# Gated linear attention and an MLP on one core: scores and running sums of two batches emitted as pairs, weights in 8 pieces instead of 12, k turned ahead of q, and a table that says which engine does each sum and copy

## The chip, the cores and the metric

The kernel runs on 1 core of a Trainium2 chip. The metric is the device time of one execution in microseconds (us). The time before is the median of 3 runs. A profile is one further execution, recorded instruction by instruction.

The engines are named as in the profile: PE is TensorE (matmuls), PEld its weight loads, DVE is VectorE, ACT is ScalarE, POOL is GpSimd, and SP is the engine whose queue issues nearly all DMAs here. SBUF is the on-chip memory of 128 partitions; PSUM holds matmul results and has 8 banks, all of which this kernel uses as one ring of eight buffers.

## What is computed

Two blocks in a row, all in float32 on the chip (the two weight matrices come as 64-bit floats and are turned into float32 by the kernel):

```python
# B, H, S, D = 4, 8, 768, 48
for t in range(S):                      # gated linear attention
    state = alpha[:, :, t, :, None] * state + k[:, :, t] (outer) v[:, :, t]
    y[:, :, t] = q[:, :, t] @ state     # 48 x 48 state per batch and head
x = y as (B, S, H * D)                  # 4 x 768 x 384
xn = (x - mean) / sqrt(var + 1e-6) * g_ln
out = x + max(xn @ w_ch1, 0) @ w_ch2    # w_ch1 384 x 1536, w_ch2 1536 x 384
```

## The kernel before

**Tiles and stages.** The 768 tokens are cut into 6 chunks of 128, so there are 24 pairs of chunk and batch. The function `attention(c, b)` does one of them: the logarithm of alpha (ACT), its running sum along the tokens as a matmul with a triangle of ones (tile `lps`, lines 330 and 335), two exponentials of it (ACT, lines 338 and 339), k and q multiplied by them (DVE, lines 341 and 343), both turned so that the head dimension lies on the partitions, the scores k·q (tile `aps`, lines 409 and 417), a masked copy of the scores (DVE, line 429), the update of the state (tile `ups`, line 445, then DVE line 458 and POOL line 460), the output (tile `yps`, line 481), the normalisation (ACT and DVE), and the turned result `xT` for the MLP. Chunk 0 works on whole 128-token blocks. The later chunks work on halves of 64 tokens, so that their matmuls are 64 wide or less and use one quarter of the TensorE array each: in a batch with an even number the two matmuls of a step use the two quarters off one diagonal, in an odd batch (`cross`) the quarters of the other one. For chunks 0 to 2, q and k are turned by TensorE (line 393, q first, then k, each followed by a copy, lines 398 and 400); from chunk 3 on by a DVE transpose and DMAs through DRAM.

**The MLP.** Chunk 0 uses plain matmuls: `hidden` (line 564, letters Y and Z of the order below, 12 column blocks `j` for each half of the batches) and `project` (line 576, letters P and Q). Chunks 1 to 5 use a scheme with fewer multiplications, in which sums of blocks are formed first: of the first weights (`combine_first`, line 802, letter S), of `xT` (`combine_x`, line 827, letter X), of the second weights (`combine_weights`, line 636, letter W) and of the hidden values (`combine_hidden`, line 663, letter N). All these sums are DVE instructions. The products are lines 853 and 676 (letters M and V); DVE, ACT and POOL add their results up.

**The weights.** They come in 12 pieces of 768 KB (6 of the first matrix, two column blocks `j` each; 6 of the second). A piece is loaded by one DMA (line 228) into one of `STAGED` = 3 staging buffers and turned into float32 in place by `round_weights`: three DVE instructions (lines 240, 242, 244), one of ACT (line 246), then DVE line 250 and either three of line 253 or one of line 256. When a piece is done, the load of piece i + 3 is issued. The letters A to L stand for the 12 pieces.

**What sets the order.** Every stage is a Python generator, and the string `ORDER` says which generator is advanced by one step next: small letters a to x are the 24 calls of `attention`, the capitals the rest. Instructions reach each engine's queue in exactly this order, and every engine, SP included, works through its queue in order. So an instruction that waits holds up all that stands behind it on its engine. In `ORDER` a batch with later chunks gives its scores in 8 steps of 2 matmuls (each float32 matmul is two TensorE instructions), and the string already mixes the steps of two batches in five of the ten pairs of batches.

```python
TURNED = 12
...
        lps = ps.tile([P, 512], FP32, name="lps", tag="bank", bufs=8)
...
    with tc.manual_schedule():
        for turn in ORDER:
            next(turns[turn], None)
```

## Time and profile before

| | us |
|---|---|
| median of 3 runs (lowest and highest) | 417.64 (416.98 to 420.2) |
| the profiled execution, whole | 418.43 |
| its span, first to last instruction | 416.6 |
| TensorE busy | 409.2 |
| VectorE busy | 344.8 |
| ScalarE busy | 182.4 |
| GpSimd busy | 151.1 |

A line of the timeline or of the chain of waits gives a start, a duration (both us) and what ran. In the timeline and in the groups, `xN` is the number of instructions, a pair like `128x512` is partitions by elements, and what stands in square brackets is how long the engine had been idle before and who ended that. "Busy" of TensorE is the time in which some matmul is under way; matmuls overlap, so a busy TensorE can still be waiting in part. The granted TensorE clock was 1.000 of full speed on average.

### The profile page before, as it was taken

Reading aid. Unit: us, or ns where it says so; the run is one execution under the profiler, and the core shown is the slowest. Engines: PE = TensorE matmul, PEld = TensorE weight load, DVE = VectorE, ACT = ScalarE, POOL = GpSimd, SP = SyncE. Lnnn points to the kernel's source line nnn. Section 1 sums busy time; section 2 is a strip of 40 time slices with the busy share of each in tenths; the row PEclk is TensorE's granted clock in tenths of the full one; section 3 lists DMA queues with packets and bytes.
Section 4 is the critical chain, followed back from the end, with each engine's and each line's share of the span. In section 5 each row is a group of like instructions: output and inputs, shape, how many; then the busy total and the mean of one; then the engine's idle time right before and its main releaser. Section 6 shows DMA issues by size and latency. Waiting matters only on the chain.

```text
span 416.6 us, 11605 instructions
## 1 busy us (share of the span) xinstructions
PE 409.2 (98%) x4628; PEld 363.2 (87%) x4628; DVE 344.8 (83%) x672; ACT 182.4 (44%) x460; POOL 151.1 (36%) x164
## 2 busy tenths in 40 slices
PE   7999899999999999999999999999999999999997
PEld 5888789866568889999889998889998899889996
DVE  3888979999999989998689779679687769857873
ACT  6599456955523585321754344174130640122300
POOL 1012020010012766026774141872136640667323
PEclk9999999999999999999999999999999999999999
DMA  8988985977866876537866785672026200100201
GB/s 266 278 258 231 254 248 151 282 228 171 231 138 152 248 163 118 123 78 189 177 135 151 184 215 146 107 170 61 24 72 171 54 24 2 57 20 1 77 19 57
DMA packets 127133, 59.69 MB, mean 143 GB/s; under 512 B 84540, under 2 KB 123196, under 8 KB 127080
## 3 DMA queue, kind: packets, MB, share of 16 engines
q1 hardware_dynamic: 126536, 58.79, 54.7%
q8 instruction: 36, 0.59, 0.6%
q10 hardware_dynamic: 544, 0.17, 0.2%
q14 instruction: 17, 0.14, 0.1%
HBM read 42.33 MB, written 16.61 MB: 141 GB/s over the span
## 4 chain that ended last, share of the span: by engine, by line
PE 88%; DMA 7%; DVE 2%; ACT 1%; SPq 0%; issue 0%; DVEq 0%
PE ops L676 31%; PE hps L853 31%; PE ops L576 8%; PE hps L564 7%; PE yps L481 4%; PE aps L417 3%; DMA gate<-row 2%; PE ups L445 2%; DMA vn<-in_v_dram 2%; DMA ws<-in_moe_w_ch_dram 1%; DMA kept<-x 1%; DMA ra<-in_alpha_dram 1%; PE lps L335 1%; PE xps L539 1%; PE tps L393 1%; ACT lps L339 0%
## 5 line engine op out<-in xcount | busy, mean ns | idle before, releaser
L692 POOL TENSOR_TENSOR ob<-ob,u 128x192 f32<-128x192 f32 x40 | 26.2, 666 | 69.9 <-DVE ob L689 55.5
L853 PE MATMUL hps<-sum,w 128*128 128x256 f32 x192 | 47.1, 380 | 0.0
L460 POOL TENSOR_TENSOR mid<-mid,gate 112x192 f32<-112x192 f32 x20 | 12.8, 643 | 86.5 <-DVE mid L458 47.4
L853 PEld LDWEIGHTS hps<-sum,w 128*128 128x128 f32 x192 | 36.3, 190 | 4.9
L676 PE MATMUL ops<-w,hT 128*128 128x192 f32 x224 | 40.4, 328 | 0.0
L676 PEld LDWEIGHTS ops<-w,hT 128*128 128x128 f32 x224 | 36.8, 190 | 0.5
L564 PE MATMUL hps<-xT,w 128*128 128x256 f32 x144 | 33.5, 383 | 1.8 <-DVE mid L458 1.8
L853 PE MATMUL hps<-xT,w 128*128 128x256 f32 x136 | 34.4, 380 | 0.0
L904 ACT ACTIVATE hT<-hT 128x512 f32<-128x512 f32 x48 | 27.9, 621 | 10.6 <-POOL hT L891 7.4
L576 PE MATMUL ops<-w,hT 128*128 128x384 f32 x96 | 32.4, 490 | 0.0
L564 PEld LDWEIGHTS hps<-xT,w 128*128 128x128 f32 x144 | 26.5, 190 | 5.5 <-issue 2.0
L853 PEld LDWEIGHTS hps<-xT,w 128*128 128x128 f32 x136 | 25.7, 190 | 3.5
L676 PE MATMUL ops<-ws,sum 128*128 128x192 f32 x160 | 28.6, 327 | 0.0
L576 PEld LDWEIGHTS ops<-w,hT 128*128 128x128 f32 x96 | 17.7, 190 | 11.4
L513 ACT ACTIVATE xn<-x,few 128x384 f32<-128x384 f32 x24 | 14.8, 615 | 28.6 <-DVE few L509 28.1
L676 PEld LDWEIGHTS ops<-ws,sum 128*128 128x128 f32 x160 | 26.4, 190 | 0.1
L676 PE MATMUL ops<-ws,hT 128*128 128x192 f32 x128 | 23.4, 326 | 0.0
L686 DVE TENSOR_TENSOR ob<-ops,ob 128x192 f32<-128x192 f32 x50 | 16.7, 349 | 7.3 <-PE ops L676 2.9
L676 PE MATMUL ops<-more,sum 128*128 128x192 f32 x120 | 21.9, 326 | 0.0
L676 PEld LDWEIGHTS ops<-ws,hT 128*128 128x128 f32 x128 | 21.3, 190 | 0.1
L460 POOL TENSOR_TENSOR st<-st,gate 112x192 f32<-112x192 f32 x16 | 10.6, 665 | 28.9 <-DVE st L458 28.9
L883 ACT COPY hT<-hps 128x512 f32<-128x512 f32 x8 | 4.7, 583 | 36.4 <-PE hps L853 36.4
(240 smaller groups left out, 1113.7 us busy)
## 6 DMA issues: line engine op xcount, KB each, us to landing
ws<-in_moe_w_ch_dram SPq DMA_DIRECT2D x12, 768.0 KB
vn<-in_v_dram SPq DMA_DIRECT2D x12, 384.0 KB
kept<-x SPq DMA_DIRECT2D x24, 192.0 KB
ob<-kept SPq DMA_DIRECT2D x24, 192.0 KB
rows<-rj SPq DMA_DIRECT2D x48, 96.0 KB
out_dram<-ob SPq DMA_DIRECT2D x19, 192.0 KB
ra<-in_alpha_dram SPq DMA_DIRECT2D x14, 192.0 KB
rk<-in_k_dram SPq DMA_DIRECT2D x6, 384.0 KB
```

The source lines that it names most:

```text
L417: nc.tensor.matmul(aps[0][halves[i if cross else 1 - i], p, s], kT[rs, p, s], qT[rs, p, s], start=True, stop=True)
L445: nc.tensor.matmul(up[h, p], qk_of(c, b)[ts, 1, p, i, :h.stop - h.start], vn[ts, i, p], start=True, stop=True)
L460: nc.gpsimd.tensor_mul(new, new, by)
L481: nc.tensor.matmul(yps[j][halves[s], i, p], of, by, skip_group_check=True, start=not (cross and k), stop=k == 1 or not cross)
L513: act(out=xn, in_=x, func=AFT.Square, bias=mean, accum_out=dev)
L564: nc.tensor.matmul(hps, w1[:, j // 2, f, j % 2 * P:][:, :P], xT_of[0][:, f, bs], start=(f == 0), stop=(f == NF - 1))
L576: nc.tensor.matmul(ops_of[b], hT_of[c][:, j, b], w2[:, j], start=(j == 0), stop=(j == NJ - 1))
L676: nc.tensor.matmul(acc, lhs[:, j], rhs[:, j], start=(j == 0), stop=(j == NT - 1))
L686: nc.vector.tensor_add(x, acc, x)
L692: getattr(nc.gpsimd, f"tensor_{op}")(x, x, y)
L853: nc.tensor.matmul(acc[:, i], w, b, start=True, stop=True)
L904: nc.scalar.activation(out=x, in_=x, func=AFT.Relu)
```

## The change

It has five parts.

1. **Pairs.** For chunks 1 to 5 the running sums of an even batch and the odd batch after it are emitted in one step (four quarter-array matmuls, eight TensorE instructions), and so are their scores (8 steps of four matmuls instead of 16 steps of two). Both batches' PSUM banks are taken at that step.
2. **Weights.** 8 pieces (`PIECES` = 4 for each matrix, three column blocks `j` each, 1,152 KB) instead of 12, with `STAGED` = 2 staging buffers instead of 3, each half as large again. `w1` is now one plain tile.
3. **Turning.** Where TensorE turns q and k, k comes first.
4. **Table.** `WHERE` gives, for each sum of W, N, X and S and for each batch's q multiplication and copies, which of two engines does it. For sums and the q multiplication 0 is DVE and 1 is POOL; for copies 0 is ACT and 1 is DVE. The ones: N 35 of 80, X 33 of 55, S 7 of 19, W 6 of 13; q multiplication 10 of 24.
5. **Order.** A new string of 1,539 letters instead of 1,646 (fewer steps and fewer pieces). Its first 39 letters are the old ones.

```diff
-STAGED = 3
+STAGED = 2
+PIECES = 4
 TURNED = 12
...
+WHERE = {
+    "N": "00000100011001011010000110110010100101100011101001010001011110100001000110101110",
+    "S": "1101100010001010000",
+    "W": "0100011110001",
+    "X": "1111011111101000001101100100010000111110101111101011110",
+    "a": "0100",
+    "b": "0100",
+    "c": "0100",
+    "d": "0001",
+    "e": "1100",
+    "f": "1000",
...
+def pick(marks, usual=0):
+    return int(marks.pop(0)) if marks else int(usual)
...
-    w1 = cpool.tile([P, NJ // 2, NF, 2 * P], FP32, name="w1")
+    w1 = cpool.tile([P, NF, DF], FP32, name="w1")
...
+    for i in range(PIECES):
+        cs = slice(i * DF // PIECES, (i + 1) * DF // PIECES)
+        pieces.append((w1[:, :, cs], w1_src[:, :, cs]))
+    for i in range(PIECES):
+        js = slice(i * NJ // PIECES, (i + 1) * NJ // PIECES)
         pieces.append((w2[:, js], w2_src[:, js]))
-    pieces = pieces[::2] + pieces[1::2]
...
         if whole:
-            nc.tensor.matmul(lps[:, :DM], tri, a, start=True, stop=True)
+            lps = ps.tile([P, 512], FP32, name="lps", tag="bank", bufs=8)
+            nc.tensor.matmul(lps[:, :DM], tri, las.pop((c, b)), start=True, stop=True)
+            yield
         else:
-            for h in range(2):
-                of = halves[1 - h if cross else h]
-                nc.tensor.matmul(lps[halves[h], :DM], tri[of, of], a[of], start=True, stop=True)
-        yield
+            if b % 2:
+                for o in (b - 1, b):
+                    sums[c, o] = ps.tile([P, 512], FP32, name="lps", tag="bank", bufs=8)
+                for o in (b - 1, b):
+                    for h in range(2):
+                        of = halves[1 - h if o % 2 else h]
+                        nc.tensor.matmul(sums[c, o][halves[h], :DM], tri[of, of], las[c, o][of],
+                                         start=True, stop=True)
+                yield
+            lps = sums.pop((c, b))
...
-        nc.vector.tensor_mul(qk[:, 0], raws.pop(("q", c, b)), eq)
+        (nc.vector, nc.gpsimd)[pick(marks)].tensor_mul(
+            qk[:, 0], raws.pop(("q", c, b)), eq)
...
-        for i in range(0 if turned(c, b) else 2):
+        for i in () if turned(c, b) else (1, 0):
...
+            if b % 2:
+                pair = [ps.tile([P, NP, 2, HS], FP32, name="aps0", tag="bank", bufs=8)
+                        for _ in range(2)]
+                scores[c, b - 1], scores[c, b] = pair
+                for p in range(NP):
+                    for s in range(2):
+                        for o in range(2):
+                            for i in range(2):
+                                rs = slice(64 * i, 64 * i + D)
+                                q_of, k_of = turned_of[c, b - 1 + o]
+                                nc.tensor.matmul(pair[o][halves[i if o else 1 - i], p, s],
+                                                 k_of[rs, p, s], q_of[rs, p, s],
+                                                 start=True, stop=True)
+                        if s == 0 or p + 1 < NP:
+                            yield
...
+    sides = {n: list(WHERE.get(n, "")) for n in "WNXS"}
+
+    def summer(name, op):
+        return getattr((nc.vector, nc.gpsimd)[pick(sides[name])], op)
...
-            op(o, x, y)
+            summer("N", op)(o, x, y)
```

More of the change, by code (lines that the diff above doesn't have):

```diff
@@ L17 @@
 EPS = 1e-6
-STAGED = 3
+STAGED = 2
+PIECES = 4
 TURNED = 12
 ORDER = (
-    "acacababcdaacabdbaabdcacabbacbbababceccbaAcfcdbadaacecacfeafdaddeedadbbbfccbeacc"
-    "fafddghdffbfcfeebbeAfefdhffaeebgeeeeeeAfbaAffbejbgdidedYcjchggifffeBdcCgAYYehdiY"
-    "ceeegghiighideefdfefhhdcghhiiiidghfhgghhcBghgghdhghBhghhgBgjggZZCZZZZYYjYCfZhifY"
-    "hkiDCBZfDDkiiCiijeiZYZklYYgggZkjYfjjjjkYkkYhjhijEZhEjiihkgljjjjjFEEFiijjFFZggZlZ"
-    "ZZZkeieiDliZlZlZlllZHZkliSklkehhhlIeilkSIklZkHljGgkllkggglfmjilkYGYYYYYYeYYejjhj"
-    "kkkjIlmGnkgGnOkYlHmmmkOHlQjnInmQSfikJJPlffPnnShJKlQKLgQnfmnhLpSfmlnKgiOLPWWWPWmh"
-    "SXoppSSooXkjSooQQQXnkkmmonXmnmnXmnniimnmnjjjSXmmnXSllnmiSOPmSmnnmpoOoPPMmppXoXmp"
-    "pmXnnnnSMSWWplnMMMMMlSMMSMMMMiMMMMXMMjlPmQlMMMMrmMMMiMOrqpppnWqoooprooppopomMppp"
-    "opqpqqMMMqqMjWlRWMjqnpMMMMRMMMMMMMMMMMMMMklRkRkkkmokWMMpMMMMRWMROrMqrrlRmRRRRorM"
-    "MMMMWMMMqooppsqmsmkNRqMqpqqqrqooooonnrOsNNNNqNKotNNNqqMosNMMMMMWoNqqNMMqMMNMMMMM"
-    "MMNpqrroMrrtttttrrrrrrrrrqoNtXtXsMMMXNXXMMXMMMXXrqqXsXMpmMMMMMsMoMoMXMMMMMMMMMMM"
-    "MMMMMppMmMMMRsMnvMMMMMnRRRuMMMtMOMMMMMMRMRMMMMMMnMMMMMMpvtspvttttotOstssttusssss"
-    "sssvRtsuttsotMMMuqqqMOrvMRpvvRMNpOMMvqMNMMMMssRssuuurRtrvsrrruRNNNNttMxNrNNMNMMM"
-    "MMMMMMrqMNNtMsNMMMMMMMMuNnMMMrMMMMwmvuuvrONNOvvuvuvvMuuuvvvuvsuwssssxuvvxwXXtuMX"
-    "XXXXMuXwMXuMMMMMsMXxtMMuttvtMwOXxxxqMMuxwuwwMMMMMwxrMMMMMMMMMMMMMMuuMMMMMMMMMMMM"
-    "MMMMtvvvvMvvRRMMMMMMMMMMMRRRMMMMxxwwxRRRRRxwvxwwxxwxwwwwwwxRxxuMMxMMRMMOsNNNNNNN"
-    "NNNNwttwwMxxxxwMMMMqMMMMMxMMMMMMMMMMNNqNNvNuMMMMuMMxxxXXXXXXXXXxMMMMMMXOMuMMxMXM"
-    "wMMMMMMMMMMMMMMMMMMMMMMMMMMMMMMMMMMMMMOOMOMMMMMMwwwwxwMMMMMMMMMMMMMMRRRRRRRuuRRR"
-    "RRNNNvNNNNwNNMMMMMMwXNMMMMNXXXXXXXXXMMMMMMMMMMMMMMMVMNMXONNVVVVVVVVVVVMVVVVVVVVV"
-    "VVVVVVVVVVLVVVVVVVVVVVVVVVVVVVVNNMVVVVVVVVVMRRMMMMMRRRRRRRRNRRNNMJOMMMMMMNNNNNNN"
-    "NMOMMMMMMOMMMMMMMMMMMMMMNNMMMNNMNMMMMMMMMMMMMM"
-)
@@ new lines @@
+    "acacababcdaacabdbaabdcacabbacbbababceccafdbccbbdafeeAdfabfddacccaeabaafaeeeebaef"
+    "ffdfdafcAdffffdffffdbbbbbgAhccAdcbhacbhggeddedBfcfccgYdhhgYdcAdYYhddYieeggejhehc"
+    "gegdedeYffjhecfjBjfjZZiiBZZZZhfBBjjjjjffhhhhhhhhhChhhggCgCYYlCeiZYZkiYZZZiiZDhZZ"
+    "iiYfYhljDjjjjjjjgjiejhhYgggYheiggEhEikDfYYlSShhgZhYYYieDkliYYYYlkefkYgkkZkggklll"
+    "lEgZiiiigllFFjSlllmjlEljllllOeefZZkijZZFZnGfZkjjZFjjnkhklmnQOmngngGhhlQkmSinmkHP"
+    "HXGHlSmSmffXXXninlpXnSSOPPPoPPPkPkWkkOmOlXpWWollllQllSWoOXXQQSXoooSSSnQSSXnnnnnn"
@@ new lines @@
+    "nnnkkkmpmmionpjQXnpnjpSWWMMMMjWnmnkMMMMMMMMmkpGMMMMqMMMMpmMmSQjoMrnrmmMrmrmrnMMk"
+    "MlMMMMrMMnWpjMMWRMMMMWqMMMMMMMMMWpRpRpppOppjpppipppmMMMkMppRMoRoRqMMMpMoqoqMiRRR"
+    "RoMMoMMRlqnnNMpNWNNqqNNOliMMMmMMMMMNNRWmNMMMMMMMMMNNNNMorrrMMMMMiMNMMMotrOsrNrrr"
+    "rrrmmMoNppqpoqqtpXqtMsXXXXnsXXoXMMoooopMssssMMMMMMtMXtttsppXMMMMMMMMMMXoMMMMMMMM"
+    "MMMMMMMrMMMqMMRRMMMMMMMMMMmMMMMMMMRRptnnRmtoqMMMMMMnMMuMOMrrqrvqqttttttOttttttRR"
+    "RRqRvNqqNNvqMqMMvvMMnNRMMsMMNNNNRtvruMoMsrtOurMMMMMMMMuNsrssutsMNtNvsrvuNtNvsxMM"
@@ new lines @@
+    "MMMNMuMNMMMMMNMMMwuXqrMsMXMMMXrMMXXXXXXxOvrvvxvvvvvvvvuquuuxrXrvqXrxxxxMMMMMMMMM"
+    "MwwwqMMMMMMwMMMMRMMMMMMMMMMMMMMMMMMMMMMMwwwMtttttvMMHMMMMMMMMMMRRRRRMRRRRMMvsxxx"
+    "xxxxNxxxxxsssusOONsxMMsMRMNMNNNNMwvtwOsMrvvvvrMNNNtRNvMMNMMMMMvMtMMMMxMMMMwxuxsw"
+    "uwuMwwwxNMuuNNNOxxwxXwwwuXXXXXXXMMXMXMMMMMMuuuMMMMMMMMMMMXxMMMMMvMMxMMMMMMMMMMMM"
+    "MRRRMMMMMMOuwvwOuMMMMMMMMRMMMMMMMMMMMMMMMMMMMxRRRxORMRRMMRwMRwNMNNNNNNMMMMMXMNMM"
+    "XXMMMXXXXXXNNNNMMMMMMMMNXXVVVVVVVVVVVVVVVVVVVVVVVVVVVVVVVVVVVVVVVVVVVVVVVVVVVMMM"
@@ new lines @@
+    "NNVVVVVVVVVRRNMRRMMMMMRRRRRRRRMMMMMMMNOMOMMNOMMOMNMNMMMMNNNNNNMNNMMMMMMMMMMMMMMM"
+    "NNNNMMMMMMMMMMMMMMM"
+)
+WHERE = {
[9 more added lines that the diff above has]
+    "f": "1000",
+    "g": "0000",
+    "h": "1001",
+    "i": "0001",
+    "j": "0000",
+    "k": "0000",
+    "l": "0010",
+    "m": "1",
+    "n": "1",
+    "o": "0",
+    "p": "0",
+    "q": "0",
+    "r": "1",
+    "s": "0",
+    "t": "0",
+    "u": "1",
+    "v": "1",
+    "w": "1",
+    "x": "1",
+}
@@ L214 @@
     pieces = []
-    for i in range(NJ // 2):
-        cs, js = slice(2 * i * P, 2 * (i + 1) * P), slice(2 * i, 2 * (i + 1))
-        pieces.append((w1[:, i], w1_src[:, :, cs]))
+    for i in range(PIECES):
[3 more added lines that the diff above has]
+        js = slice(i * NJ // PIECES, (i + 1) * NJ // PIECES)
         pieces.append((w2[:, js], w2_src[:, js]))
-    pieces = pieces[::2] + pieces[1::2]
     staged = {}
@@ L251, in round_weights @@
             op1=AOP.bitwise_or)
-        for f in range(NF) if i < NJ // 2 else ():
+        for f in range(NF) if i < PIECES else ():
             stt(out=dst[:, f], in0=dst[:, f], scalar=g_col[:, f:f + 1], in1=hi[:, f].bitcast(FP32),
                 op0=AOP.mult, op1=AOP.mult)
-        if i >= NJ // 2:
+        if i >= PIECES:
             stt(out=dst, in0=dst, scalar=2.0 ** -20, in1=hi.bitcast(FP32), op0=AOP.mult, op1=AOP.mult)
@@ L264, in take_weights @@
         else:
-            for f in range(NF) if i < NJ // 2 else ():
+            for f in range(NF) if i < PIECES else ():
                 nc.scalar.mul(pieces[i][0][:, f], pieces[i][0][:, f], g_col[:, f:f + 1])
@@ L304 @@
         nc.gpsimd.memset(at, 0.0)
-    x_of, xT_of, hT_of, las = ({} for _ in range(4))
+    x_of, xT_of, hT_of, las, turned_of, scores, sums = ({} for _ in range(7))
     def attention(c, b):
         whole, last = c == 0, c + 1 == NCB
+        marks = list(WHERE.get(chr(ord("a") + c * B + b), ""))
+        copies = (nc.scalar.copy, nc.vector.tensor_copy)
         cross = b % 2 and not whole
@@ L326, in attention @@
         yield
-        lps = ps.tile([P, 512], FP32, name="lps", tag="bank", bufs=8)
-        a = las.pop((c, b))
         if whole:
-            nc.tensor.matmul(lps[:, :DM], tri, a, start=True, stop=True)
-        else:
-            for h in range(2):
-                of = halves[1 - h if cross else h]
-                nc.tensor.matmul(lps[halves[h], :DM], tri[of, of], a[of], start=True, stop=True)
-        yield
+            lps = ps.tile([P, 512], FP32, name="lps", tag="bank", bufs=8)
+            nc.tensor.matmul(lps[:, :DM], tri, las.pop((c, b)), start=True, stop=True)
+            yield
+        else:
+            if b % 2:
[8 more added lines that the diff above has]
+            lps = sums.pop((c, b))
         lv = lps[:, :DM].rearrange("t (i p d) -> t i p d", i=2, d=D)
@@ L367, in turned_tiles @@
         def turned_tiles():
-            return [work.tile([R, NP, 2, HS], FP32, name=n, tag="sum", bufs=12)
-                    for n in ("qT", "kT")]
+            turned_of[c, b] = [work.tile([R, NP, 2, HS], FP32, name=n, tag="sum", bufs=12)
+                               for n in ("qT", "kT")]
+            return turned_of[c, b]
         if not turned(c, b):
@@ L396, in attention @@
             tv = tps.rearrange("r p (s t) -> r p s t", s=2)
-            if i:
-                (nc.vector.tensor_copy if whole else nc.scalar.copy)(out=kT, in_=tv)
-            else:
-                nc.scalar.copy(out=qT, in_=tv)
+            copies[pick(marks, whole and i)](out=kT if i else qT, in_=tv)
             yield
-        aps = [ps.tile([P, NP, 2, HS], FP32, name=f"aps{i}", tag="bank", bufs=8)
-               for i in range(2 if whole else 1)]
-        for p in range(NP):
-            if whole:
+        if whole:
+            aps = [ps.tile([P, NP, 2, HS], FP32, name=f"aps{i}", tag="bank", bufs=8)
+                   for i in range(2)]
+            for p in range(NP):
                 for i in range(2):
@@ L412, in attention @@
                                      start=True, stop=True)
-                continue
-            for s in range(2):
-                for i in range(2):
-                    rs = slice(64 * i, 64 * i + D)
-                    nc.tensor.matmul(aps[0][halves[i if cross else 1 - i], p, s],
-                                     kT[rs, p, s], qT[rs, p, s], start=True, stop=True)
-                if s == 0 or p + 1 < NP:
-                    yield
-        yield
+        else:
+            if b % 2:
+                pair = [ps.tile([P, NP, 2, HS], FP32, name="aps0", tag="bank", bufs=8)
+                        for _ in range(2)]
+                scores[c, b - 1], scores[c, b] = pair
+                for p in range(NP):
+                    for s in range(2):
[8 more added lines that the diff above has]
+                            yield
+        if whole or b % 2:
+            yield
         if whole:
@@ L430, in attention @@
                 out=at.rearrange("k p s t -> k (p s) t"),
-                data=aps[0].rearrange("k p s t -> k (p s) t"),
+                data=scores.pop((c, b)).rearrange("k p s t -> k (p s) t"),
                 mask=mask_of_halves.unsqueeze(1).broadcast_to([P, 2 * NP, HS]))
@@ L540, in attention @@
         yield
-        nc.scalar.copy(out=xT_of[c][:, :, b], in_=xps)
+        copies[pick(marks)](out=xT_of[c][:, :, b], in_=xps)
         yield
@@ L563, in hidden @@
         for f in range(NF):
-            nc.tensor.matmul(hps, w1[:, j // 2, f, j % 2 * P:][:, :P], xT_of[0][:, f, bs],
+            nc.tensor.matmul(hps, w1[:, f, j * P:(j + 1) * P], xT_of[0][:, f, bs],
                              start=(f == 0), stop=(f == NF - 1))
@@ L616, in weights_ready @@
         return win["b"]
+    sides = {n: list(WHERE.get(n, "")) for n in "WNXS"}
+    def summer(name, op):
+        return getattr((nc.vector, nc.gpsimd)[pick(sides[name])], op)
     def combine_weights():
-        spare = [stage.tile([P, NF, 2 * P], INT64, name="ws", tag="ws") for _ in range(3)]
+        spare = [stage.tile([P, NF, NF * P], INT64, name="ws", tag="ws") for _ in range(STAGED)]
         spare = [t.rearrange("p a c -> p (a c)").bitcast(FP32) for t in spare]
         new = [t[:, i * NT * HM:][:, :NT * HM].rearrange("p (j m) -> p j m", m=HM)
-               for t in spare for i in range(2)] + [
+               for t in spare for i in range(3)] + [
             more[:, i].rearrange("p (j m) -> p j m", m=HM) for i in range(4)]
@@ L625, in combine_weights @@
         t8, t9, t12, t1, n0, n6, n2, n13, n5, n10 = new
-        add, sub = nc.vector.tensor_add, nc.vector.tensor_sub
+        add, sub = "tensor_add", "tensor_sub"
         ready = weights_ready()
@@ L635, in combine_weights @@
                 ((13,), sub, n13, t8, b[4])):
-            op(o, x, y)
+            summer("W", op)(o, x, y)
             ready |= {n: o for n in ns}
@@ L650, in combine_hidden @@
             work.tile([P, NT, P], FP32, name=f"sum{i}", tag="sum", bufs=12) for i in range(6))
-        add, sub = nc.vector.tensor_add, nc.vector.tensor_sub
+        add, sub = "tensor_add", "tensor_sub"
         for n, op, o, x, y in (
@@ L662, in combine_hidden @@
                 del ready[old]
-            op(o, x, y)
+            summer("N", op)(o, x, y)
             ready[n] = o
@@ L757, in product, with w1_block @@
         yield
+    def w1_block(t, f):
+        return w1[:, f, t * NT * P:(t + 1) * NT * P].rearrange("p (a c) -> p a c", a=2)
     def first_weights_ready():
         if "a" not in first_of:
-            first_of["a"] = {n: [w1[:, 2 * t:2 * t + 2, f]]
+            first_of["a"] = {n: [w1_block(t, f)]
                              for n, t, f in ((7, 2, 1), (10, 1, 0), (13, 0, 1), (8, 0, 0))}
@@ L780, in combine_first @@
         extra = cpool.tile([P, 6 * P], FP32, name="extra")
-        a = [[w1[:, 2 * t:2 * t + 2, f]] for t in range(3) for f in range(NF)]
+        a = [[w1_block(t, f)] for t in range(3) for f in range(NF)]
         spare = [raw.tile([P, 2, 2, NP, D], FP32, name=f"r{n}", tag="in", bufs=6).rearrange(
@@ L785, in combine_first @@
         n9, n1 = ([x[:, 4 * P:].unsqueeze(1) for x in spare[2 * i:2 * i + 2]] for i in range(2))
-        add, sub = nc.vector.tensor_add, nc.vector.tensor_sub
+        add, sub = "tensor_add", "tensor_sub"
         ready = first_weights_ready()
@@ L801, in combine_first @@
             for o, u, w in zip(out, parts(x, len(out)), parts(y, len(out))):
-                op(o, u, w)
+                summer("S", op)(o, u, w)
             if n is not None:
@@ L817, in combine_x @@
         t101, t103, t100, m7, t102, m10, m9, m13, m8 = new[:9]
-        add, sub = nc.vector.tensor_add, nc.vector.tensor_sub
+        add, sub = "tensor_add", "tensor_sub"
         ready = x_ready(c)
@@ L826, in combine_x @@
                 (8, sub, m8, t102, b[1])):
-            op(out, x, y)
+            summer("X", op)(out, x, y)
             if n is not None:
```

## Prediction, made before the changed kernel was run

> **What bounds the kernel now.** I read the page's busy times first, then TensorE's waits, then the chain of waits in order of time, and then the timeline at the places that the change touches.

> ```profile
> PE 409.2 (98%) x4628; PEld 363.2 (87%) x4628; DVE 344.8 (83%) x672; ACT 182.4 (44%) x460; POOL 151.1 (36%) x164
> PE hps L564 <- DVE mid L458: 1.8, 1, 1.8
> PE tps L393 <- DVE qk L343: 1.3, 1, 1.3
> PE lps L276 <- DVE more L273: 1.1, 1, 1.1
> PE aps L409 <- ACT qT L400: 0.2, 1, 0.2
> ```

> TensorE is busy for 98% of the span, and all its waits come to 4.4 us, each at one place. Nothing else can be the bound: VectorE has 72 us to spare, GpSimd 265. So time can only come from TensorE's own work, from those 4.4 us, and from work that goes badly together on the array. The last can be read from the chain (start, duration, what):

> ```profile
> 86.02 0.64 PE lps L335 x4
> ...
> 108.95 0.81 PE lps L335 x8
> ...
> 116.04 1.09 PE aps L417 x64
> ...
> 141.02 0.87 PE aps L417 x35
> ...
> 213.18 0.74 PE aps L417 x26
> ...
> 279.45 1.08 PE aps L417 x60
> ```

> The blocks of 60 and 64 are two batches whose steps the order already mixes: 17 to 18 ns for one instruction. The blocks of 26 and 35 are a batch by itself: 28 and 25 ns. Running sums by themselves take 0.64 us for one batch, 0.81 us for two. Each change between full-array and quarter-array matmuls also costs:

> ```profile
> 115.55 0.49 PE L576 MATMUL ops<-w,hT 128*128 128x384 f32 x1
> 115.97 1.16 PE L417 MATMUL aps<-qT,kT 48*64 48x64 f32 x64
> ```

> The block starts 0.42 us after the matmul before it, where 384 columns follow each other every 0.32 us (40 in 13.10 us, chain at 87.13): 0.1 us. Back again, starts in the trace show 0.1 us at the last small matmul and 0.1 at the first big one. One change is 0.15 us on average.

> **The change part by part**, against the profiled execution (418.43 us: span 416.6 and 1.8 around it, 0.8 above the median of the three runs, 417.64).

> *Scores as pairs.* The same 640 instructions. Five of ten pairs are mixed already. For the other five, 320 instructions at 26.5 less 17.5 ns give 2.9 us. But the old order puts single running sums between single scores, on the other diagonal of the array: at 178.27 to 179.25, 32 scores and 4 sums take 0.98 us, and at pair prices they would take 32 x 17.5 ns + 0.81/2 = 0.97. Nothing is to be had there. Group by group (starts in the trace against pair prices) the excess is 0.7 us at 25 to 29, 0.4 at 32, 0.6 at 139, 0.1 to 0.2 in five others: 2.4 in all, part of it waits. I take -2.0, ends 0 and -2.9. In this the running sums are neutral: five single pairs of them would save 5 x (1.28 - 0.81) = 2.4 if they stood alone, and cost 5 x 0.81 = 4.0 if the old ones were wholly hidden; 178.27 says in the middle.

> *The order.* Expanding both strings step by step, TensorE changes between full and quarter array 52 times before and 46 times after: 6 x 0.15 = -0.9 (ends -0.5 and -1.2).

> *k ahead of q.* At 9.78 TensorE waits 1.3 us for line 343, the multiplication of q, which stands behind that of k (0.56 us, from 8.33; q from 9.17). Turning k needs the first alone. In the first chunk k's copy is on DVE and q's on ACT as before. -0.5 (ends 0 and -0.6). Late next: the scores still need both copies.

> *Weights, first piece.* Its rounding on DVE and ACT before:

> ```profile
> 25.07 0.54 DVE L240 TENSOR_SCALAR w<-ws 128x768 int32<-128x768 int32 x1
> 25.64 0.96 DVE L242 SCALAR_TENSOR_TENSOR w<-ws,w 128x768 f32<-128x768 uint32 x1
> 26.63 0.56 DVE L244 TENSOR_SCALAR ws<-ws 128x768 int32<-128x768 int32 x1
> 27.65 0.48 DVE L519 TENSOR_SCALAR xn<-x,few 128x384 f32<-128x384 f32 x1 [0.46 <-ACT few L516]
> 28.57 0.96 DVE L250 SCALAR_TENSOR_TENSOR ws<-ws 128x768 int32<-128x768 int32 x1 [0.44 <-ACT ws L246]
> 29.66 1.28 DVE L253 SCALAR_TENSOR_TENSOR w<-w,small,ws 128x256 f32<-128x256 f32 x3
> ```

> It is done at 30.94, and the first hidden product starts at 30.60 on the part that is ready. The piece had landed at 21.3 by the semaphore records, so 3.7 us lay between. A piece half as large again takes 3.1 us instead of 2.1 on the DMA engines (the second one came 2.1 us after the DMA ahead of it), and on SP's queue its issue moves behind the second gate column and the row of batch d (0.4 and 0.5 us): it lands at about 23.4, when VectorE comes to it. Its chain grows from 5.9 to about 8.4 us, so it is done at 31.8. The first product stands at the same place of TensorE's work (priced by the rows above, 22.4 us after the first running sum, as before), so it would start at 30.5. Also the normalised x of batch b (line 519) now stands behind the piece's first three instructions, and TensorE turns it just before. I take +1.2, ends 0 and +4.

> *The wait of 1.8 us at 43.9.* TensorE waits for a PSUM bank there: the multiply-out of a state sum (line 458) that frees it stands on DVE behind the second piece's rounding, and that had waited for its load (landed 39.8). In the new order the second piece's load is issued ahead of d's k, q and v work, it has 15 us until the next column blocks need it, and no bank is taken at that place within 1.2 us of its release. -1.8 (ends -1.8 and 0).

> *Weights, later pieces.* 24 DVE instructions and 4 of ACT fewer, but VectorE has time to spare: 0. The second matrix is wanted earlier: `project` needs all of its last third some 7 us sooner in TensorE's work than before, and by the same reckoning (4.4 us load and 1.05 more, a chain of 8.4) the seventh piece is done about when it is wanted, at 98 us. +0.7, ends 0 and +3.

> *The table.* On VectorE a sum of 128x512 takes 0.68 us, of 128x256 0.42, on GpSimd 128x512 takes 1.27 and 128x192 0.59; between these lie about 0.73 for 256, 1.0 for 384, and beyond them 1.8 for 768 elements (estimates on the straight line through these two rows). VectorE loses 35 x 0.68 + 33 x 0.42 + 7 x 0.68 + 6 x 0.95 + 10 x 0.57 = 54 us, GpSimd gains 35 x 1.27 + 33 x 0.73 + 7 x 1.27 + 6 x 1.8 + 10 x 1.0 = 98 and stands at 249 of 416. Neither is a bound. But they hinder each other:

> ```profile
> 375.90 1.28 POOL L878 TENSOR_TENSOR at<-ra,rq 128x512 f32<-128x512 f32 x1
> 377.25 1.60 POOL L879 TENSOR_TENSOR at<-at,at 128x512 f32<-128x512 f32 x1
> 376.18 1.55 DVE L663 TENSOR_TENSOR sum<-sum,hT 128x512 f32<-128x512 f32 x1
> 377.76 1.64 DVE L663 TENSOR_TENSOR sum<-sum,sum 128x512 f32<-128x512 f32 x1
> ```

> The 0.68 us sums took 1.55 and 1.64 beside GpSimd. What is queued behind a GpSimd sum is the state's multiplication (line 460), which the output matmuls need. The distances in the order between a sum and its product are as before (1.3 us at the least in both). +0.5, ends -0.5 and +8.

> Sum: -2.0 - 0.9 - 0.5 + 1.2 - 1.8 + 0.7 + 0.5 = -2.8. The profiled execution would take 415.6 us, the median 414.8.

> **The rivals.**

> *Clean.* No new stall: -2.9 - 0.9 - 0.5 - 1.8 = -6.1, 411.5 us. For it: in the old profile TensorE waits for nothing after 46 us, although sums stood 1.3 us from their use; banks in use at once go from 8 to 7 at most. Against it: 8.4 us for the first piece.

> *The pairs bring nothing*, and the stall only moves: 417.3 us (-0.9 + 0.6). For it: half the pairs and most sums are mixed already. [...] The trace disagrees: 64 columns at 0.84 ns (0.323 us for 384) are 54 ns, a batch alone ran at 25 to 28 and a pair at 17. So pairs are faster where they are new.

> *GpSimd becomes the late one* (slower). Place: the 36 state multiplications of line 460, each with output matmuls waiting. If a sum of 1.27 us stands in front and TensorE has nothing else, each costs 1.27. Without the table the rest brings -3.3, so from 3 such places on the kernel is slower than before, and from 6 on by over 1%; eight give 10.2 - 3.3 = +6.9, 424.5 us. For it: GpSimd goes from 36% to 60%, and the pair of 1.6 us lines. Against it: the multiplication's wait today ends with VectorE, not with GpSimd's queue. [...]

> *The first piece is 4 us late*: 417.6 us. It needs the landing after 26 us.

> **How the numbers follow.** Forecast 0.45, clean 0.24, no gain 0.15, GpSimd 0.12, late piece 0.04. The prediction is the likeliest, 414.8 us. 1%, about what a measurement of this kernel can tell from no change, is 4.2 us: faster by that is below 413.5, slower above 421.8. Clean counts as faster, and 0.12 of the forecast's lower side: 0.36. GpSimd is slower nearly whole, with a little of the others: 0.13. The rest, 0.51, is the same. The range: clean's better half and GpSimd's worse half left out, 411.2 to 420.5; the forecast's own range is 412.9 to 416.5.

> **What would show it.** Scores: blocks of 64 at 17 to 18 ns everywhere, lps in blocks of eight of 0.8 us. Order: the sums of slots after 125 us shorter by about 1.5 us. k first: the wait at 9.78 gone, first turn at about 9.1. First piece: a wait of TensorE at line 564 or at the turning of batch b between 27 and 32. Bank wait: no wait of line 564 near 44. Seventh piece: a wait at line 576 near 98. Table: VectorE near 290 to 310 us, GpSimd near 250 to 280, line 460 waited for by yps. I am wrong if TensorE's waits after 46 us exceed 4 us, or if its busy time falls by more than 6.

## The result, and the profile after

| | before | after |
|---|---|---|
| median (lowest and highest), us | 417.56 (416.98 to 420.2) | 423.67 (422.99 to 424.92) |
| span of the profiled execution, us | 416.6 | 423.1 |
| granted TensorE clock, mean | 1.000 | 0.996 |

Four runs each on one chip: the changed kernel takes 1.0128 times as long (95% interval 1.0084 to 1.0173), 6 us more, where the prediction had 2.8 less. One kernel below (after with 64 more instructions) was profiled in a long execution, 432.56 us: its median of 426.35 counts it, its ratio leaves it out, and of its trace the argument uses the places of the pauses and the grid of the clock.

Busy times, from the page of after:

```profile
PE 409.9 (97%) x4628; PEld 360.2 (85%) x4628; DVE 313.6 (74%) x561; ACT 179.4 (42%) x452; POOL 251.0 (59%) x255
```

The same matmuls, the same busy time to 0.7 us; VectorE and GpSimd moved the way the table says. So 5.8 of the 6.5 us of span are idle time of TensorE (13.2 us outside its busy time, 7.4 before). Its waits in after (line, who ended the wait, us in total, times, longest):

```profile
PE aps L467 <- issue: 4.3, 1, 4.3
PE lps L313 <- DVE more L310: 1.1, 1, 1.1
PE yps L533 <- DVE ob L632: 1.0, 2, 0.8
PE lps L368 <- ACT la L363: 0.7, 2, 0.5
PE yps L523 <- issue: 0.7, 1, 0.7
PE yps L533 <- issue: 0.6, 1, 0.6
```

The largest wait, and two more, end with "issue": no semaphore ended them. The chain in order of time shows the largest, in the middle of a block of scores:

```profile
46.96 0.71 PE aps L467 x46
47.67 4.27 issue
51.93 0.49 PE aps L467 x15
52.43 1.51 PE ups L497 x52
53.93 3.11 PE hps L616 x9
```

No input can be missing for the other scores of the same block: they had all been there before it began. Two clues say what is. Of the DMA queues, the page of after has

```profile
q1 hardware_dynamic: 125704, 58.79, 53.6%
q8 instruction: 36, 0.59, 0.6%
```

36 packets of 0.59 MB in all, 16,384 bytes each; and TensorE's records (matmuls, weight loads, semaphore instructions) are 9,367, one packet for each 256. Ahead of the pause stand 1,473 of them, five groups of 256 and 193. The other two pauses that end with "issue" (0.87 us at 26.94, 0.77 at 67.35) also stand behind the 193rd instruction of a group, and so does the wait of before at 43.53, which the page of before puts down to VectorE's line 458. The packet's times, from the trace: it started at 49.41 and was there at 50.55; the scores went on at 51.93, 1.38 later. In before: 43.21, 44.29, and TensorE went on at 45.69, 1.40 later.

The DMA queues of after in the stretch 49.4 to 50.56, that of this packet, and before it the issues from 40.3 to 49.38:

```profile
q1 hardware_dynamic: 275, 0.40, 99.1%
q8 instruction: 1, 0.02, 6.1%
```

```profile
q1 hardware_dynamic: 1475, 2.37, 87.4%
q14 instruction: 1, 0.01, 0.2%
issues: line engine op xcount, KB each, median us to landing
ws<-in_moe_w_ch_dram SPq DMA_DIRECT2D x2, 1152.0 KB
```

Of the issues the first line is shown. The DMA engines carried data for 87.4% of those 9 us, and no TensorE packet passed. The third weight piece had been issued at 42.20 (landed 48.59) and the next chunk's alpha at 42.69 (landed 49.39); TensorE began the last 256 instructions ahead of the pause at 42.19. The packet came just behind them.

The pause has a price behind it. Stretches of after, with the granted clock (PEclk) in the third column from the right:

```profile
46.90:47.70 0.80, 0.77 (x51) 0.63 (x43) 0.80 (x2) 0.80 (x5) 0.00 (x0) 1.00 0.98 366
47.70:51.90 4.20, 0.00 (x0) 0.00 (x0) 0.87 (x2) 0.25 (x2) 0.00 (x0) 1.00 1.07 326
51.90:53.90 2.00, 1.97 (x83) 1.87 (x82) 1.43 (x2) 0.00 (x0) 0.00 (x0) 0.64 1.06 367
53.90:56.20 2.30, 2.30 (x8) 1.92 (x7) 2.23 (x3) 0.00 (x0) 0.00 (x0) 0.57 0.50 35
56.20:60.00 3.80, 3.80 (x19) 3.34 (x19) 3.25 (x6) 2.99 (x6) 0.51 (x1) 1.00 0.00 0
```

After the pause the clock was 0.64 and 0.57 on average in two stretches, 4.3 us together; within them it was 0.50 from 52.46 to 55.86 and 1.00 outside. The matmuls of line 616 started every 425 ns, not every 216, and 52 of line 497 took 1.51 us, where a run without the pause (below) has 58 in 0.91: by the starts, about 1.5 us in all.

The account of the 6.5 us of span, from the starts in the two traces: pauses for packets 6.1 instead of 2.2 (+4.0); half speed behind the long one (+1.5); a wait for VectorE at 115.8 (+1.4, below); one at 94.9 where the turned x waits for VectorE (+0.5); 3.4 us instead of 2.8 between the last matmul and the end (+0.6). That is +8.0, so 1.5 us are left as what the change saves in TensorE's work; this is a remainder, not a measurement.

The wait at 115.8, as the timeline of after shows it on VectorE and GpSimd:

```profile
112.05 4.58 DVE L862 TENSOR_TENSOR w<-w 128x512 f32<-128x512 f32 x1 [1.17 <-POOL w L862]
116.55 1.01 DVE L632 TENSOR_TENSOR ob<-ops,ob 128x384 f32<-128x384 f32 x2
```

```profile
111.97 0.97 POOL L512 TENSOR_TENSOR st<-st,gate 112x192 f32<-112x192 f32 x2
112.89 0.73 POOL L887 TENSOR_TENSOR sum<-sum,sum 128x256 f32<-128x256 f32 x1
113.58 1.82 POOL L693 TENSOR_TENSOR ws<-w 128x768 f32<-128x768 f32 x1
115.35 0.73 POOL L887 TENSOR_TENSOR sum<-sum,xT 128x256 f32<-128x256 f32 x1
116.03 1.17 POOL L887 TENSOR_TENSOR sum<-xT 128x256 f32<-128x256 f32 x1
```

A VectorE sum that takes 0.69 us elsewhere took 4.58 beside an unbroken row of GpSimd instructions; the addition behind it (line 632) frees the banks that the output matmuls of line 533 need.

### The profile page after: what moved, and what is told of

Its sections match the earlier page's. It is cut to its first block, busy times and chain, and to the rows that moved or that the text cites. A ratio compares the mean times of both kernels' runs of the same rounds, so it can differ in the third digit from the quotient of the medians.

```text
span 423.1 us, 11620 instructions
## 1 busy us (share of the span) xinstructions
PE 409.9 (97%) x4628; PEld 360.2 (85%) x4628; DVE 313.6 (74%) x561; ACT 179.4 (42%) x452; POOL 251.0 (59%) x255
## 4 chain that ended last, share of the span: by engine, by line
PE 89%; DMA 3%; DVE 3%; issue 3%; POOL 1%; SPq 1%; POOLq 0%; DVEq 0%
PE hps L913 31%; PE ops L733 30%; PE ops L628 7%; PE hps L616 6%; PE yps L533 4%; PE ups L497 3%; PE tps L439 2%; PE aps L467 2%; DMA ws<-in_moe_w_ch_dram 2%; DMA rq<-in_q_dram 1%; PE lps L377 1%; PE yps L523 1%; PE aps L452 1%; PE xps L591 1%; DVE w L277 1%
## 5 line engine op out<-in xcount | busy, mean ns | idle before, releaser
L512 POOL TENSOR_TENSOR mid<-mid,gate 112x192 f32<-112x192 f32 x20 | 13.1, 658 | 29.7 <-DVE mid L510 21.3
L616 PEld LDWEIGHTS hps<-xT,w 128*128 128x128 f32 x144 | 27.4, 196 | 3.7
L913 PEld LDWEIGHTS hps<-xT,w 128*128 128x128 f32 x136 | 25.7, 190 | 4.0 <-DVE at L481 0.6
L733 PEld LDWEIGHTS ops<-ws,sum 128*128 128x128 f32 x160 | 26.5, 190 | 0.1
L565 ACT ACTIVATE xn<-x,few 128x384 f32<-128x384 f32 x24 | 14.8, 616 | 26.9 <-DVE few L561 26.5
L533 PE MATMUL yps<-st,qT 48*64 48x48 f32 x320 | 20.5, 221 | 1.5 <-DVE ob L632 1.0
L533 PEld LDWEIGHTS yps<-st,qT 48*64 48x64 f32 x320 | 16.9, 133 | 5.9 <-issue 2.8
L363 ACT ACTIVATE la<-ra 128x384 f32<-128x384 f32 x24 | 12.1, 518 | 22.2 <-DMA ra<-in_alpha_dram 22.2
```

The costliest lines, as they stand in the source:

```text
L363: nc.scalar.activation(out=la, in_=raws.pop(("a", c, b)), func=AFT.Ln)
L512: nc.gpsimd.tensor_mul(new, new, by)
L533: nc.tensor.matmul(yps[j][halves[s], i, p], of, by, skip_group_check=True, start=not (cross and k), stop=k == 1 or not cross)
L565: act(out=xn, in_=x, func=AFT.Square, bias=mean, accum_out=dev)
L616: nc.tensor.matmul(hps, w1[:, f, j * P:(j + 1) * P], xT_of[0][:, f, bs], start=(f == 0), stop=(f == NF - 1))
L733: nc.tensor.matmul(acc, lhs[:, j], rhs[:, j], start=(j == 0), stop=(j == NT - 1))
```

## The experiments

Theory F: TensorE's pauses are waits for its own instructions, in packets of 256, which stand behind data in the DMA engines. Rivals: the matmuls wait for a PSUM bank, a copy or VectorE (B); the time is lost by table and order on the engines (R); the packet's delay is its own (L). Theory S: GpSimd's sums hold VectorE's up. Ratios are to the kernel before, run beside it on the same chip.

**64 more instructions in the warm-up, after and before.**

```diff
-    for _ in range(8):
+    for _ in range(4):
         nc.tensor.matmul(idle[:, :P], zero, zero, start=True, stop=True)
+    for _ in range(20):
+        nc.tensor.matmul(idle[:32, :32], zero[:, :32], zero[:, :32], start=True, stop=True)
```

> The changed kernel with 64 more TensorE instructions in the warm-up ahead of the work (4 large and 20 tiny matmuls on zeros in place of 8 large); the work itself is the same, in the same order. Theory F (TensorE waits for its own instructions: they arrive in packets of 16,384 bytes, one for each 256 instructions, and every stall without a releaser in both traces stands right behind instruction 193 of such a group): the group borders move by 64 instructions against the work. The stall of 4.48 us at 47.45 goes, because its packet is asked for 64 instructions, some 3 us, earlier; with it goes the stretch of half-speed matmuls at 53.9 (1.5 us). The stalls of 0.87 us at 26.94 and 0.77 at 67.35 leave these instructions. New ones, if any, stand behind 193 of a group and are under 1.5 us. Median 417 to 419.5 us. Rival B (those matmuls wait for a PSUM bank, for the copies of kT, or for the dense array work itself): the 4.5 us stall stays at the same score matmul, 257 instructions from no border; median 423 to 424.5.

> The kernel before with the same 64 more TensorE instructions in its warm-up. Theory F: the stall of 2.16 us at 43.53 to 45.69 at the first-layer matmul of chunk 0 goes, although VectorE's work is the same, since it too stands behind instruction 193 of a group; a new one is likeliest at about 65 us, where 256 instructions of work would pass in 2.5 us, and would be 1 to 2 us. Median 415.5 to 418. Rival B, the prediction's own reading (the matmul waits for a PSUM bank that VectorE's multiplication frees late): the wait stays at the same matmul within 0.5 us of its length; median 417.6 within 0.7.

Measured: after 426.35 us, ratio 1.0128 (1.0069 to 1.0188); before 419.82, ratio 1.0009 (0.9973 to 1.0045). The places came out as F says and the times did not. In after the pause in the scores is gone, and five others stand, all behind instruction 193 of a group: 3.39 us at 37.76 in the state's matmuls, 0.76 at 68.28, 2.10 at 89.67, 2.27 at 240.69, 1.63 at 310.15. The expectation allowed less than 1.5 each: the packets were later than in the run from which that was taken. In before the wait at 43.53 is gone too, and the row of matmuls runs through:

```profile
41.49 4.80 PE L566 MATMUL hps<-xT,w 128*128 128x256 f32 x21
```

while what the prediction took for the cause came later on VectorE:

```profile
42.95 1.28 DVE L253 SCALAR_TENSOR_TENSOR w<-w,small,ws 128x256 f32<-128x256 f32 x3
44.14 0.35 DVE L460 TENSOR_TENSOR mid<-ups,st 112x192 f32<-112x192 f32 x1
```

The matmul that had waited in before started at 42.89 here, 1.6 us before the state's addition (line 460 here, 458 in before) ended at 44.49. So it does not wait for that addition; in before the addition had merely ended 0.03 us ahead of it:

```profile
45.38 0.28 DVE mid L458
45.66 0.03 issue
45.69 1.46 PE hps L564 x6
```

Instead a pause of 2.65 us came at 63.33 (expected at about 65, 1 to 2), in the state's matmuls:

```profile
63.21 0.33 PE ups L447 x10
63.54 2.44 issue
65.98 0.44 PE ups L447 x12
```

Two shorter ones, 0.63 and 0.70 us, stand at 164 and 168. The median, 419.82, lies above the 415.5 to 418 that F gave, so a pause that goes in one place and comes in another saves nothing.

What follows: the pauses belong to the count of instructions, not to the work. B falls for both kernels.

**The third piece's load behind the next chunk's.** In `ORDER` the letter A at place 141 goes behind the h at 145 (a piece of the string):

```diff
-gYdcAdYYhddYi
+gYdcdYYhAddYi
```

> The changed kernel with the load of the third weight piece issued behind the next chunk's alpha, k and q loads of batches 2 and 3, not ahead of them. Theory F with a queue: the instruction packet of the 4.48 us stall started 7 us after its group was entered because 0.8 MB of weights and then alpha were ahead of it on the DMA engines; without the weights it starts at 45 to 47 instead of 49.4, and the stall is 0 to 1.8 us. Median 418.5 to 421.5. Rival L (the packet's delay is its own and does not depend on what is ahead): the stall stays 4 to 5 us, median 423 to 425. The rounding of that piece may come up to 3 us later, which either theory leaves open.

Measured: 425.98 us, ratio 1.0152 (1.0101 to 1.0202). The packet started at 45.83 and the pause was 1.74, both inside what F gave; L is out. But the time stayed: VectorE now waits for the piece, and TensorE behind it:

```profile
53.53 1.36 DVE w L277
54.89 0.02 issue
54.92 1.37 DVE w L279
56.28 0.02 issue
56.31 0.76 DVE ws L281
57.07 0.28 DVE mid L510
57.34 0.04 issue
57.39 1.13 PE hps L616 x4
```

a wait of 3.83 us from 53.56, with half speed behind it. The expectation left that open; the median missed its range.

**All sums and q multiplications on VectorE.** All of N, S, W, X zero, and the first mark of e, f, h, m, n, r, u to x.

```diff
...
-    "S": "1101100010001010000",
+    "S": "0000000000000000000",
...
```

> The changed kernel with all sums (weights, hidden rows, first-layer blocks, inputs) and all multiplications of q on VectorE, as before the change; copies stay where the new table puts them. Theory S (GpSimd's sums hold VectorE's up: a 0.69 us sum took 4.58 us at 112.05, and TensorE then waited 1.3 us at 115.84 for the addition behind it): that wait goes, and the tail after the last matmul (3.6 us against 3.0) shortens; the 4.48 us stall at 47.45 stays as it is. Median 421 to 422.5. Rival V (VectorE, back to about 345 us busy, becomes late in the new order, whose due times were set for the table): new waits for VectorE after 100 us, median 424 to 428.

Measured: 426.99 us, ratio 1.0166 (1.0118 to 1.0215). S is right in its place: the wait at 115.8 is gone. V is right in the median: TensorE waits 1.1 us at 104.9 for a late rounding on VectorE. Another wait of 1.7 us at 141.5 ends with a load of alpha that SP issued only at 139.25; whether VectorE had held SP up is not shown. The pause of 4.48 us stands unchanged, and the half speed behind it covers 4.4 us of work, not 3.4, which is 0.5 us more. The end after the last matmul takes 2.9 us instead of 3.4. So the table costs 1.4 us at 115.8 and about 0.5 at the end, and saves 1.1 at 104.9. The two ratios overlap (1.0166 here, 1.0128 in after): the table is no clear loss here, and no shown gain.

**A third of each weight load.**

```diff
...
-        nc.sync.dma_start(dst, src)
+        nc.sync.dma_start(dst[:, :1], src[:, :1])
...
```

> The changed kernel, but each weight load moves only a third of its piece (the other two thirds of the staged piece are zeros set at the start); rounding and all later work run on whole pieces as before. It leaves out two thirds of the weights, so that less is ahead of the instruction packets on the DMA engines. Theory F with a queue: the packet that came at 49.41 starts about 2 us sooner for the load of its own moment and more for those ahead, the 4.48 us stall falls below 1.5, the half-speed stretch behind it goes, the stalls behind instruction 193 of a group come to 0 to 2 us instead of 6.1; profiled span 414 to 418, median 415 to 419. Rival R (the change costs its time by the table and the order, on the engines): the median stays within 2 us of 424.

> The kernel before with the same cut: each weight load moves a third of its piece, the rest zeros. Theory F: the 2.16 us wait at 43.53 shrinks below 0.5; median 414.5 to 416.5, so that the two kernels with a third of the loads stand within 2.5 us of each other, where whole loads leave 6. Rival R: the difference of the two stays 5 to 6 us. The prediction's reading (a PSUM bank behind VectorE's rounding, which waits for its load) would also let the wait go here; the run with shifted instructions has told these apart.

Measured: after 418.23 us, ratio 0.9991 (0.9953 to 1.0030); before 417.26, ratio 0.9949 (0.9933 to 0.9966). Six us between the two kernels became one by the medians (1.8 by the ratios, whose intervals overlap). In after no pause for a packet is left: the one of the scores started at 40.60, 8.8 us sooner, and the block runs through:

```profile
44.20 1.08 PE yps L536 x64
45.28 0.95 PE aps L470 x64
46.23 0.91 PE ups L500 x58
```

In before the packet started at 41.82 and 1.20 us of 2.16 stayed (expected under 0.5: missed). R falls: with the load on the DMA engines gone, table and order leave 1 to 2 us, not 6; 1.3 of them are the wait behind VectorE's sum, here at 107.7. The waits for weights go as well in both kernels, so this is not the packets' price to the tenth.

**Scores of a pair one after the other.**

```diff
-                        for o in range(2):
+                for o in range(2):
+                    for n in range(NP):
...
+                        for p, s in ((n, 0), (n, 1)):
...
```

> The changed kernel with the scores of the two batches of a pair one after the other (first four steps the one batch, last four the other) in place of both in turn; instructions, steps and running sums are the same. If pairs are worth what the prediction took (9 ns for each of the 640 instructions, as all ten pairs would run unmixed): 5 to 6 us more, 428.5 to 430, blocks of 32 at 25 to 28 ns. Rival (they bring nothing, since weights and moving data of one batch overlap as well): within 0.7 us of the changed kernel, blocks still at 17 ns. The stall behind the border in the scores at 47.45 stays in either.

Measured: 429.37 us, ratio 1.0249 (1.0203 to 1.0296): 0.0121 of 419.27 above the changed kernel's ratio, 5.1 us. A block without its pair, and the same one in after:

```profile
64.88 1.64 PE aps L467 x59
```

```profile
65.85 0.93 PE aps L467 x64
```

28 ns an instruction against 15. By the median it is 8 ns for each of the 640 instructions, where the prediction took 9, and the rival falls. The median understates it, because the pause in the scores was 3.41 us here, not 4.48 as expected, and the two shorter ones were gone, 2.7 us less in all. Added up from each start to the next in the traces (without the pauses), the 640 score instructions take 16.8 us here and 10.4 in after: 10 ns each.

**Sums of the first weights on VectorE, and 12 more instructions.** S all zeros; three tiny matmuls behind the eight.

> The changed kernel with the 19 sums of first-layer blocks back on VectorE, and 12 more tiny TensorE instructions in the warm-up. Theory S: the 4.58 us sum at 112 and the wait of 1.3 us at 115.84 go. Theory F: all borders move by 12 instructions, each stall stands at the new border; from the packets' delays in the runs so far I work out 0.4 us at 26.7, 3.6 at 46.5, 0.4 at 62, 1.7 at 66.5, 6.1 in all as before. Median 421.5 to 423. Rival V (VectorE late instead, as with all sums on it, where new waits of 1.1 us at 104.9 and 1.7 at 141.5 came): 424 to 426.

Measured: 423.93 us, ratio 1.0115 (1.0070 to 1.0161), above the expected 421.5 to 423. S in this form is wrong: the wait stayed (1.62 us at 113.52), and VectorE's sums beside GpSimd's other sums were slow too, 5.42 us for two:

```profile
109.19 5.42 DVE L864 TENSOR_TENSOR w<-w 128x512 f32<-128x512 f32 x2
```

Pauses for packets came to 6.5 us (expected 6.1), all behind instruction 193: 1.50 at 39.53, 3.13 at 46.87, 1.87 at 64.49. The total and the one at 46.9 were about right; the others stand at borders for which less or nothing was expected.

**Both loads moved.** A from place 141 to 135; the load of the next chunk by h behind the fourth piece's (place 192).

> The changed kernel with two loads moved on SP's queue: the third weight piece is issued ahead of the row of batch h and of the kept x of batch d (about 40 us, not 42.2), and the next chunk's alpha, k and q of batches 2 and 3, which nothing reads before 58 us, behind the fourth weight piece (about 48.7, not 42.7). Theory F with a queue: only the weight piece is then ahead of the packet asked for at 42.2; it starts at 44.5 to 46.5 instead of 49.4, the 4.48 us stall falls to 0 to 1.5, and without so long a pause the half-speed stretch of 1.5 us goes; unlike the load moved later, rounding is not late. Median 3.5 to 6 us under the changed kernel, 418.5 to 421 beside a before of 418.5. Rival L (loads are late for their users in the new places): new waits at 58 to 62 us for alpha or k, median 422 to 425.

**The same, with ten sums of X and one of W back on VectorE.**

```diff
-    "W": "0100011110001",
-    "X": "1111011111101000001101100100010000111110101111101011110",
+    "W": "0000011110001",
+    "X": "0000000000001000001101100100010000111110101111101011110",
```

> As the kernel with the two loads moved, and 11 sums that GpSimd made near 112 us (ten of the inputs of chunk 1, one of the second weights) back on VectorE. Theory S, as the last run leaves it: the 4.58 us sum is held up by whatever sums GpSimd makes beside it, not by those of its own kind; with these gone it takes under 2 us and the wait of 1.3 us at 115.84 goes: 1 to 1.7 us under the kernel with the loads moved alone, about 417 to 419.5. Rival V: VectorE has 4 to 5 us more ahead of the last rounding (wait of 1.1 us at 104.9 with all sums on it) and nothing is won.

Measured: 421.54 us, ratio 1.0046 (1.0009 to 1.0082), and 419.47, ratio 1.0002 (0.9963 to 1.0042), beside a before of 419.42. In the first the packet started at 45.62, the moment when the data ahead of it was through (batch d's x landed at 45.70), the pause is 1.47, and no half-speed stretch follows. The median is 0.5 us above the expected range, and this run's rival L is in part right: the next chunk's alpha, issued at 49.48, landed at 56.52, ScalarE's logarithm of it stood ahead of a copy, and TensorE waited 1.03 us at 56.44 for that copy. In the second the wait at 115.8 is gone, and the sum takes its usual time:

```profile
108.96 0.68 DVE L871 TENSOR_TENSOR w<-w 128x512 f32<-128x512 f32 x1
```

Two hand-made moves, one for each cause, take the loss from 1.28% to 0.46% to none; the intervals of the last two overlap, so that step rests on the trace, in which the wait is gone, more than on the medians. Two pauses for packets are left in it (1.74 us at 46.27, and 1.86 at 62.46 with half speed behind). It does not beat the kernel before.

**q ahead of k again.**

```diff
-        for i in () if turned(c, b) else (1, 0):
+        for i in () if turned(c, b) else (0, 1):
...
```

> The changed kernel with q turned ahead of k again; the engines of the copies stay as the table has them for each of the two. The prediction's term: 0.5 us more, with the first turn back at about 9.6 to 9.8 behind the multiplication of q. Rival (the gain is lost at once, since the scores still wait for the second copy: 0.53 us at 12.33 in the changed kernel): the first score stands at the same time within 0.2 us, and the median within 0.7 us of the changed kernel's 424.

Measured: 424.1 us, ratio 1.0086 (1.0048 to 1.0124), which overlaps that of after (1.0128). The first score stands at 11.96, in after at 11.34; so k first does gain 0.6 us there, and then waits 0.53 for kT's copy at 12.33. In the median nothing of it shows, but that does not mean that k first is worth nothing. The pause in the scores was 0.82 here, not 4.48 (the packet started at 45.34), and the two shorter ones were gone: 5.3 us less. In their place TensorE waited 0.85 us at 43.84 and 2.21 at 55.84 for q's multiplication (line 387) and 2.08 at 81.17 for kT's copy, 5.1 us that after does not have. How much of that is the price of q first, and how much comes from TensorE arriving there earlier, this run does not separate.

**200 more instructions in the warm-up of before** (6 large and 52 tiny).

> The kernel before with 200 more TensorE instructions in the warm-up (6 large and 52 tiny matmuls on zeros). Theory F, with the packets' delays of the two runs of this order so far laid over the work: no stall behind a border before 160 us (the 2.16 us at 43.53 gone and none in its place), one of 1.6 us at about 163 and one of 0.3 at 223. Median 0 to 2 us under the kernel before, if the longer warm-up (some 4 us of tiny matmuls) does not push the first running sums back; by that up to 1 us more.

Measured: 423.96 us, ratio 1.0092 (1.0056 to 1.0127): wrong in size. The pauses were 1.27 us at 42.63 in the scores, 0.67 at 77.84, 1.29 at 167.94 and 2.08 at 229.26, and the first turn came 1.4 us later. Where a pause stood followed from the count, instruction 193 of a group in all of them; how long it was went with the data ahead (in the scores of after 4.48 us with all loads, none with a third of each weight load), and delays taken from other executions did not foretell it.

Over all 14 traces, 30 pauses of over 0.45 us (after the first 9 us) stand right behind instruction 193 of a group. They end 1.30 to 1.82 us after the packet's end, 1.45 in the middle. Outside half-speed stretches no pause of that length without a releaser stands anywhere else.

## Why the prediction was wrong

- **What bounds the kernel** (TensorE's own work and its few waits): right. That all its waits come from semaphores: wrong, and with it the sum, which has no term for instructions.
- ***The wait of 1.8 us at 43.9*** is the step that failed. It took the releaser that the page names, line 458, as the cause, and booked -1.8 since the new order frees the bank in time. The matmul waited for its packet: with 64 instructions more it ran 1.6 us before line 458 was through. Its successor stands at the same place of the count, 1473, at 47.45, and is 4.48 us long, as 1,152 KB of weights and the next chunk's loads now stand ahead of the packet. With the two shorter pauses and the half speed behind the long one this step is off by 7.3 us: +5.5 (+4.0 and +1.5) where it has -1.8.
- ***The table***: the term was +0.5 and measured 1.4 at 115.8 and most of the 0.6 at the end (with all sums on VectorE the end was 2.9 us, not 3.4). VectorE's busy time fell by 31 us, not by the 54 of the term's row sums: its TENSOR_TENSOR instructions took 22 us over their median times in after, 8 in before. What the rows ahead of it show, VectorE sums slowed beside GpSimd, is what came, at another size: 1.55 and 1.64 us there for a sum of 0.68, 4.58 us here for one of 0.69. The rival had the wrong queue: not the state's multiplication on GpSimd was late, but an addition on VectorE. The longest GpSimd instruction beside the sum took 1.82 us, less than the 3.9 that the sum lost. The sum ended at 116.62, 0.55 us after the fifth of them; why it lasted past the first, no run shows.
- ***Scores as pairs***, ***the order***, ***k ahead of q***: -2.0, -0.9 and -0.5, together -3.4; the account leaves -1.5. Added up from each start to the next, the score instructions take 14.5 us in before and 10.4 in after, those of the running sums 5.1 and 7.2. So the pairs bring -4.1 and +2.1, -2.0 together: the term is right in its total, by luck in part, since the running sums were taken as neutral and the scores' gain as 2.9 at most. For the order and k first the account leaves +0.5 instead of -1.4; which of the two fell short is not settled. k's 0.6 us in the first chunk is nearly lost again at kT's copy.
- ***First piece***, +1.2: no wait of line 616 or of batch b's turning between 27 and 32. A pause of 0.87 at 26.94 stands there, for a packet: the size is near by chance, the cause was another, and in the account the pause stands under the packets.
- ***Later pieces***, +0.7: 0.5 us at 94.9, where the turned x waits behind VectorE's rounding. About right.
- The terms add up: -2.8 forecast, and 7.3 for the packets, 1.5 for the table, 1.9 for the three gains, less 1.2 and 0.2 for the pieces, make the 6.5 of the spans.
- Of the signs: blocks of 64 scores at 15 to 18 ns, sums in eights of 0.8 us, POOL 251, first turn at 9.06 and no wait of the first layer near 44 came as said; VectorE was 313.6, just over 310. "Waits after 46 us above 4" was named as what would make it wrong, and did.

Behind the pause of 4.48 us the clock was 0.50 for 3.41 us. Pauses of 1.86 us (both loads moved, sums on VectorE) and 2.10 us (after with 64 more instructions) had half-speed stretches behind them too, and 2.16 (before) and 2.65 (before with 64 more) had none, so the length alone does not decide here.

The clock records of the traces show what went with it. All half-speed stretches ahead of a run's end last 3.41 us (one 6.83), and within one execution they start whole multiples of 3.413 us apart: 52.45 and 424.51 in after (109 of them), 42.08, 93.28 and 243.46 in after with 64 more instructions (15 and 44). With the trace cut on that grid, each 3.41 us that was followed by half speed held 1.64 us or more without matmul or weight load; after 1.49 us or less none followed. The 2.16 us of before were split by such a border, with 1.49 on the longer side. One stretch with 1.82 us (before with 64 more) was still followed by full speed, so the limit is not sharp, and no run was made to test it.

What stays open: why the border is at 193 and what sets the 1.3 to 1.8 us after the packet's end; and how much shorter the pauses would be with the same bytes in smaller loads, which was not tried.

## What to carry to other kernels

A pause of a busy engine whose end no semaphore explains, or only one that ended a moment before by chance, is worth counting: number its instructions, and compare with the packets of the queue that carries instructions (q8 here). Here a dense stretch (256 matmuls and weight loads, most of them small, in 5 us) met a burst of large loads, and the program itself came late, with a pause of 4.48 us that was 1.47 with two of the loads moved; so a load that nobody needed yet was not free even if it was early. And the sums and multiplications moved to GpSimd did not take off VectorE what they weigh (31 us for 54 by their rows): look at the VectorE sums that stand beside unbroken rows of GpSimd, where one took 4.58 us for 0.69.
